# Attention row sums on one Trainium2 core: the last 64 keys added by GpSimd instead of multiplied by TensorE

## Chip, core and metric

The kernel runs on one core of a Trainium2 chip. The metric is the device time of one execution in microseconds (us), here 455.82, the median of 3 runs (454.74 to 456.12). Engines are named as in the profile: PE is TensorE's matmul, PEld its weight load, ACT is ScalarE, DVE is VectorE, POOL is GpSimd, SP is SyncE.

## What is computed

```python
scores = cap * np.tanh(scale * np.matmul(q, k.transpose(0, 1, 3, 2)) / cap)   # 8 batches x 12 heads, 448 x 448, head size 64
attn = np.exp(scores - max)
attn = attn / (np.sum(attn, axis=-1, keepdims=True) + 1e-09)
x = np.matmul(attn, v)                      # then reordered to 3584 tokens x 768
idx = np.argmax(x @ w_gate, axis=1)         # 8 experts
for e in range(8):                          # the 80 tokens of expert e with the largest gate weight
    out[tok] = gate_w[tok] * (np.maximum(x[tok] @ w1[e], 0.0) @ w2[e])
```

## The kernel before

Attention is cut into 24 units of four heads: two pairs `pr` of two heads `h`. Keys lie on the partitions and queries on the free axis. Of a head's 448 keys, three chunks of 128 fill the partitions. The last 64 keys would fill only half of them, so their exps are folded (`rest_of`, L1154): the first 224 queries stand on partitions 0 to 63, the other 224 on partitions 64 to 127. All exps of a unit lie in one tile `e`: slots 0 and 1 hold the folded rests of both pairs, the next twelve the chunks.

The program is one list of steps. The 25 passes of the loop `for w in range(NU + 1)` (L1488) run the scores and exps of unit w and, interleaved with them, the values and sums of unit w-1. I call such a pass step w. Its order is written out by hand in the string `STEPS` (L1470); `FIRST` and `LAST` are the lists of the first and the last step.

- `q0` to `q6` (`scores`, L1160): `q0` multiplies the folded rests, `q1` to `q6` one chunk of one pair each. Every score pass ends with a tanh on ACT (L1180), which reads the two-bank buffer `sc`. There are two such buffers.
- `e3`, `e0`, `e1`, `e2` (`expo`, L1182): the exps of slots `RUNS`, in place, on ACT (L1184). `e3` is the rests, `e0` and `e1` hold pair 0 and the first chunk of pair 1, `e2` the last two chunks of pair 1.
- `p00`, `p01`, `p10`, `p11` (`esum`, L1186): POOL adds the three chunks of a pair into a tile `t` of 128 partitions x 2 heads x 448 queries, two chunks first (L1191), then the third (L1194), one instruction of 448 elements for each head. The pool of `t` has three buffers.
- `v0` to `v6` (`av`, L1205): passes over the previous unit. A pass works on two halves of 64 rows at once (`half`, L1196): rows 0 to 63 and rows 64 to 127 of the array each multiply 64 keys into a bank of their own, `av_0`, `av_1` or `sp`. `PASSES` (L1473) names them. In `v3` rows 0 to 63 and in `v4` rows 64 to 127 sum the tiles `t` into `sp` with matmuls against ones ("s" there, L1213); the first of them in `v3` is where PE first needs the tiles.
- `r0`, `r1`, `r2` (`rests`, L1233): the last 64 keys, with 224 queries a matmul. Rows 0 to 63 give the first half of the queries, rows 64 to 127 the second. A pass multiplies either by `v` into an `av` bank (L1246) or by ones into `sp` (L1244): `r0` is av_0 and `sp`, `r1` is `sp` and av_1, `r2` is av_1 and av_0.
- `s` (`sums`, L1249) on DVE transposes `sp` and takes reciprocals; `n0`, `n1` (`scaled`, L1262) multiply the `av` banks by them, which frees these banks for the next `v0`.
- `b` (`background`) places pieces of the routing (gates, ranks, lists of tokens) between the steps. A planner with a clock of its own decides how many; `PLACE` (L51) tells it what time the six places of a step stand for.

```python
f = ((0, None), (None, 1), (1, 0))[part][i]
if f is None:
    behind(nc.tensor.matmul(st["sp", u][...], ones[w, 0:32], e, start=(part == 0), stop=False))
else:
    behind(nc.tensor.matmul(st["av", u, f][...], last_of(u, pr, h, i)[w, 32 * f:32 * f + 32], e, ...))
```

Unit 23 (`DIRECT`) has no tiles `t`: its chunks are summed by PE (`total_of`). After attention, from about 327 us on, the experts' matmuls stream 84 loads of weights.

Of the kernel before, what the change touches and what calls it, by code (L numbers as in the profile page):

```python
# [7 lines left out]
F32 = mybir.dt.float32  # L8
# [3 lines left out]
ALU = mybir.AluOpType  # L12
# [4 lines left out]
B, H, S, D = 8, 12, 448, 64  # L17
# [3 lines left out]
CK = 128  # L21
# [26 lines left out]
WPRE = 8  # L48
WMORE = 10
DIRECT = (23,)  # L50
PLACE = (2650, 1500, 1500, 1880, 2250, 1880)  # L51
SUMS = (1500, 6200)
VALUES = (1880, 2650)
LASTPLACE = (3950, 6200, 2650, 1300, 1300, 1300)
# [11 lines left out]
HQ = S // 2  # L66
# [54 lines left out]
def attn_moe(ctx, tc, q2, k, v, cap, wg, w1, w2, capacity, ct, out):  # L121
    nc = tc.nc
# [15 lines left out]
    ones = consts.tile([128, 128], F32, name="ones")  # L138
# [951 lines left out]
    st = {"laid": set(), "banks": ["misc"], "held": {}, "take": None, "read": 0, "late": False}  # L1090
# [29 lines left out]
    with ExitStack() as a2:  # L1120
        ep = a2.enter_context(tc.tile_pool(name="ep", bufs=2, reuse_waits="tile"))
        tp = a2.enter_context(tc.tile_pool(name="tp", bufs=3, reuse_waits="tile"))
# [28 lines left out]
        def last_of(u, pr, h, i):  # L1151
            return st["v", u][:, pr, h, NK] if h == i else st["vx", u][:, pr]

        def rest_of(u, pr, h):  # L1154
            return st["e", u][:, h, HQ * pr:HQ * pr + HQ]

        def chunk_of(u, pr, c, h):
            return st["e", u][:, 2 + 2 * NK * pr + 2 * c + h]

        def scores(u, x):  # L1160

            if ("e", u) not in st:
                st["e", u] = ep.tile([CK, 2 + 4 * NK, S], F32, name=f"e{u}", tag="e")
            ps = pss.tile([CK, 2, 512], F32, name=f"sc{u}_{x}", tag="sc")
            if x == 0:
                for pr in range(2):
                    for m in range(4):
                        for h in range(2):
                            w = slice(64 * h, 64 * h + 64)
                            i, y = m // 2, NK * CK * (1 - h) + 32 * (m % 2)  # L1170
                            nc.tensor.matmul(ps[32 * m:32 * m + 32, h, HQ * pr:HQ * pr + HQ], st["k", u][w, pr, y:y + 32], st["q", u][w, pr, HQ * i:HQ * i + HQ],  # L1171
                                             start=True, stop=True)
            else:
                pr, c = divmod(x - 1, NK)
                for m in range(4):
                    for h in range(2):
                        w = slice(64 * h, 64 * h + 64)
                        y = KR * h + c * CK + 32 * m
                        nc.tensor.matmul(ps[32 * m:32 * m + 32, h, :S], st["k", u][w, pr, y:y + 32], st["q", u][w, pr], start=True, stop=True)  # L1179
            nc.scalar.activation(st["e", u][:, 2 * x:2 * x + 2], ps[:, :, :S], AF.Tanh, scale=st["regs"][0])  # L1180

        def expo(u, x0, x1):  # L1182
# [2 lines left out]

        def esum(u, pr, i):  # L1186
            e = st["e", u][:, 2 + 2 * NK * pr:2 + 2 * NK * (pr + 1)]
            if i == 0:
                t1 = st["es", u, pr] = tp.tile([CK, 2, S], F32, name=f"t1{u}_{pr}", tag="t1")
                for h in range(2):  # L1190
                    nc.gpsimd.tensor_tensor(t1[:, h], e[:, h], e[:, 2 + h], op=ALU.add)  # L1191
            else:
                for h in range(2):
                    nc.gpsimd.tensor_tensor(st["es", u, pr][:, h], st["es", u, pr][:, h], e[:, 4 + h], op=ALU.add)  # L1194

        def half(u, i, what):  # L1196

            w = slice(KR * i, KR * i + KR)
            if what == "s":
                return [(st["sp", u], ones[w, 0:32], st["es", u, g // 2][w, g % 2], False, i == 1) for g in range(4)]  # L1200
            f, c = what
            return [(st["av", u, f], st["v", u][w, g // 2, g % 2, c, 32 * f:32 * f + 32], chunk_of(u, g // 2, c, g % 2)[w],
                     c == 0 and f == i, c == NK - 1 and f != i) for g in range(4)]

        def av(u, n):  # L1205

            if n == 0:
                for f in range(2):
                    st["av", u, f] = psa.tile([128, 512], F32, name=f"av{u}_{f}", tag=f"av{f}")
            todo = [half(u, i, x) for i, x in enumerate(PASSES[n]) if x != "s" or u not in DIRECT]  # L1210
            for g in range(4):
                for ps, v_, e, first, final in [x[g] for x in todo]:
                    behind(nc.tensor.matmul(ps[32 * g:32 * g + 32, :S], v_, e, start=first, stop=final))  # L1213

        def behind(mm):

            if st.get("turned"):
                tc.add_manual_dep(mm.ins, st.pop("turned").ins.name, SYNC, reason="rows of the array change banks")
            st["mm"] = mm
# [13 lines left out]
        def rests(u, part):  # L1233

            if part == 0:
                st["sp", u] = ps1.tile([128, 512], F32, name=f"sp{u}", tag="sp")
            for g in range(4):
                pr, h = divmod(g, 2)
                for i in range(2):
                    w = slice(KR * i, KR * i + KR)  # L1240
                    f = ((0, None), (None, 1), (1, 0))[part][i]
                    e = rest_of(u, pr, h)[w]
                    if f is None:
                        behind(nc.tensor.matmul(st["sp", u][32 * g:32 * g + 32, HQ * i:HQ * i + HQ], ones[w, 0:32], e, start=(part == 0), stop=False))  # L1244
# [222 lines left out]
            nc.tensor.matmul(ready[:, 0:128], ones, ones, start=True, stop=True)  # L1467
        guards()
        setup()
        STEPS = ("q0 q1 e3 v0 r0 b q2 v1 b q3 e0 v2 x b q4 p00 r1 v3 x b q5 e1 v4 s v5 p01 l b q6 e2 r2 v6 p10 p11 n0 n1 b").split()  # L1470
        FIRST = "q1 q2 q3 e0 q4 p00 q5 e1 p01 l q6 e2 p10 p11 q0 e3".split()
        LAST = ("v0 r0 q v1 v2 b x q r1 v3 t x q s b v4 v5 r2 v6 n0 n1 b q b q b q b").split()
        PASSES = (((0, 0), (1, 0)), ((0, 1), (1, 1)), ((0, 2), (1, 2)), ("s", (0, 0)), ((1, 0), "s"), ((1, 1), (0, 1)), ((1, 2), (0, 2)))  # L1473
        TURNS = (0, 1, 2, 3, 4, 5, 6)
# [13 lines left out]
        for w in range(NU + 1):  # L1488
# [7 lines left out]
            if w == NU:  # L1496
                transfers(w)
                st["gates"] = None
            todo = FIRST if w == 0 else STEPS if w < NU else LAST
            st["late"] = w == NU  # L1500
            left = 1 + -w % NQ
            for i, x in enumerate(todo):
                k_ = x[0]
                a_ = [int(y) for y in x[1:]]
                if k_ == 'q' and w < NU:
                    scores(w, TURNS[a_[0]])
                elif k_ == 'q':
                    begin()
# [176 lines left out]
```

## Time and profile before

| what | value |
|---|---|
| median of 3 runs | 455.82 us |
| the profiled execution's own time | 456.44 us |
| its span, first to last instruction | 454.7 us |
| granted clock of TensorE, mean | 0.987 |
| busy: PE, ACT, POOL, DVE | 432.4, 331.4, 246.4, 233.8 us |
| bytes moved, mean rate | 101.22 MB, 223 GB/s |

The profile shows one execution. Its time beside the span is 456.44 - 454.7 = 1.74 us. Busy shares are taken over the whole span, and they mix attention (up to about 327 us) with the experts. What a change in a step of attention is worth has to be read from that step: which engine waits there, for whom, and which wait ends last. On PE eight matmuls run side by side (two row halves by four column groups of 32), so a matmul's own duration is longer than the time that a pass of sixteen takes; the pace of PE is read from the starts of the passes. ACT and POOL instructions of one engine overlap a little too, so their pace is also read from start to start.

### The profile page before, as it was taken

The page shows a single profiled execution, that of the slowest core. Times are in us where ns is not written, and L with a number is a line of the kernel's source. Part 1 is how long each engine was busy: PE and PEld are TensorE (multiplying, and loading weights), DVE is VectorE, ACT ScalarE, POOL GpSimd, SP SyncE. Part 2 cuts the span into 40 slices and gives each one's busy share as a digit, 9 for nine tenths or more (in the row PEclk, how much of TensorE's full clock was granted, in tenths as well). Part 3 has the DMA queues.
Part 4 walks back from the last instruction along what each step waited for, and adds up shares of the span by engine and source line. Part 5 has one row for each costly group of instructions (what it writes and reads, how often), then busy time and mean ns, then how long its engine had stood idle before and what let it go on. Part 6 is the DMA issues. An engine that isn't in the chain of part 4 may idle for free.

```text
span 454.7 us, 21513 instructions
## 1 busy us (share of the span) xinstructions
PE 432.4 (95%) x9533; PEld 230.3 (51%) x9533; DVE 233.8 (51%) x756; ACT 331.4 (73%) x386; POOL 246.4 (54%) x277
## 2 busy tenths in 40 slices
PE   7899999999999999999999999999899999989990
PEld 4344544654444444445444544544346766677680
DVE  1033345337534563776259897977855886210002
ACT  5999989989998988897889988879601154257142
POOL 1767766767765675765576766857655110331000
PEclk9899999999999999999999999999999999999996
DMA  6667695697769559863834862874839997999961
GB/s 158 176 176 203 198 268 160 180 288 211 204 179 269 155 162 276 234 187 99 229 88 133 219 176 82 245 207 147 241 107 360 409 414 275 308 368 410 411 253 38
DMA packets 70549, 101.22 MB, mean 223 GB/s; under 512 B 15264, under 2 KB 52896, under 8 KB 70448
## 3 DMA queue, kind: packets, MB, share of 16 engines
q1 hardware_dynamic: 69072, 96.31, 67.9%
q0 software_dynamic: 752, 3.26, 2.3%
q8 instruction: 77, 1.26, 1.2%
q10 hardware_dynamic: 624, 0.18, 0.2%
q14 instruction: 24, 0.20, 0.1%
HBM read 76.13 MB, written 23.90 MB: 220 GB/s over the span
## 4 chain that ended last, share of the span: by engine, by line
PE 75%; DVE 10%; DMA 7%; ACT 3%; issue 2%; POOL 1%; SPq 1%; POOLq 0%; DVEq 0%; ACTq 0%
PE av L1213 22%; PE sc L1179 22%; PE hp L865 6%; PE yp L865 5%; PE sp L1213 4%; PE av L1246 3%; PE sc L1171 3%; DMA w<-in_w_dram 2%; PE sp L1244 2%; PE lgp L1292 2%; DVE gb L515 2%; DMA xge<-xs,gi 1%; PE pd L447 1%; PE hp5a L865 1%; DMA vr<-in_v_dram 1%
## 5 line engine op out<-in xcount | busy, mean ns | idle before, releaser
L1180 ACT ACTIVATE e<-sc 128x896 f32<-128x896 f32 x168 | 150.9, 913 | 31.1 <-PE sc L1179 28.8
L1213 PE MATMUL av<-e,vr 64*32 64x448 f32 x2304 | 164.5, 538 | 2.0 <-DMA vr<-in_v_dram 1.2
L1179 PE MATMUL sc<-qt,kt 64*32 64x448 f32 x2304 | 143.6, 544 | 3.1 <-ACT e L1180 2.7
L1191 POOL TENSOR_TENSOR t<-e 128x448 f32<-128x448 f32 x92 | 104.7, 1159 | 75.1 <-ACT e L1184 75.1
L1184 ACT ACTIVATE e<-e 128x1792 f32<-128x1792 f32 (+1 forms) x96 | 144.7, 1507 | 0.8
L1194 POOL TENSOR_TENSOR t<-t,e 128x448 f32<-128x448 f32 x92 | 104.5, 1158 | 31.9 <-ACT e L1184 31.9
L1213 PEld LDWEIGHTS av<-e,vr 64*32 64x32 f32 x2304 | 54.4, 107 | 61.6 <-issue 40.6
L1179 PEld LDWEIGHTS sc<-qt,kt 64*32 64x32 f32 x2304 | 42.2, 106 | 47.3 <-issue 32.3
L1254 DVE STREAM_TRANSPOSE st<-sp 128x448 f32<-128x448 f32 x24 | 15.6, 650 | 68.4 <-PE sp L1213 65.2
L1246 PE MATMUL av<-e,vr 64*32 64x224 f32 x384 | 46.6, 349 | 0.0
L1213 PE MATMUL sp<-t,ones 64*32 64x448 f32 x368 | 45.2, 536 | 0.0
L901 POOL DMA_INDIRECT out_dram<-ysv,si x6 | 6.7, 1111 | 69.2 <-ACT ysv L900 62.6
L865 PE MATMUL hp<-w,xt 128*32 128x256 f32 x720 | 41.7, 380 | 1.1 <-DVE xt L693 1.1
L865 PE MATMUL yp<-w,thv 128*32 128x192 f32 x960 | 40.8, 326 | 1.7 <-DMA w<-in_w_dram 1.7
L1246 PE MATMUL av<-e,vx 64*32 64x224 f32 x384 | 42.1, 349 | 0.0
L900 ACT ACTIVATE ysv<-yp,gq 32x192 f32<-32x192 f32 x60 | 24.8, 413 | 16.3 <-PE yp L865 7.9
L865 PEld LDWEIGHTS yp<-w,thv 128*32 128x32 f32 x960 | 32.0, 110 | 9.1 <-issue 2.5
L1266 DVE TENSOR_TENSOR x<-av,r 128x448 f32<-128x448 f32 x48 | 27.7, 618 | 14.4 <-PE av L1213 14.4
L865 PEld LDWEIGHTS hp<-w,xt 128*32 128x32 f32 x720 | 23.5, 110 | 16.3 <-issue 2.3
L1246 PEld LDWEIGHTS av<-e,vr 64*32 64x32 f32 x384 | 22.4, 107 | 16.6 <-issue 15.7
L441 DVE TENSOR_SCALAR_CACHE_REDUCE gb<-krow,kc 112x896 bf16<-112x896 f32 (+7 forms) x36 | 29.8, 871 | 0.6 <-PE pd L447 0.6
L1244 PE MATMUL sp<-e,ones 64*32 64x224 f32 x384 | 28.4, 349 | 0.0
(254 smaller groups left out, 443.0 us busy)
## 6 DMA issues: line engine op xcount, KB each, us to landing
w<-in_w_dram SPq DMA_DIRECT2D x36, 512.0 KB, 8.5
w<-in_w_dram SPq DMA_DIRECT2D x48, 384.0 KB, 8.1
vr<-in_v_dram SPq DMA_DIRECT2D x24, 512.0 KB, 3.9
out_dram<-zero SPq DMA_DIRECT2D x14, 768.0 KB, 5.4
xs<-xb SPq DMA_DIRECT2D x32, 336.0 KB, 6.2
kt<-in_k_dram SPq DMA_DIRECT2D x46, 224.0 KB, 5.4
qt<-in_q_dram SPq DMA_DIRECT2D x46, 224.0 KB, 5.3
vx<-in_v_dram SPq DMA_DIRECT2D x48, 32.0 KB, 3.7
```

The source lines that it names most:

```text
L441: nc.vector.tensor_scalar(g, krow[:, x:y], kp, 0.0, op0=ALU.is_ge, op1=ALU.add, accum_out=a)
L865: nc.tensor.matmul(spot(ps, g, q)[32 * j:32 * j + 32], of(g), w[:, q * j:q * j + q], start=(kk == 0 and g % 2 == 0), stop=(kk == last and ...
L900: nc.scalar.activation(dst, src, AF.Copy, scale=gate(g))
L1179: nc.tensor.matmul(ps[32 * m:32 * m + 32, h, :S], st["k", u][w, pr, y:y + 32], st["q", u][w, pr], start=True, stop=True)
L1180: nc.scalar.activation(st["e", u][:, 2 * x:2 * x + 2], ps[:, :, :S], AF.Tanh, scale=st["regs"][0])
L1184: nc.scalar.activation(e, e, AF.Exp, scale=st["regs"][1])
L1191: nc.gpsimd.tensor_tensor(t1[:, h], e[:, h], e[:, 2 + h], op=ALU.add)
L1194: nc.gpsimd.tensor_tensor(st["es", u, pr][:, h], st["es", u, pr][:, h], e[:, 4 + h], op=ALU.add)
L1213: behind(nc.tensor.matmul(ps[32 * g:32 * g + 32, :S], v_, e, start=first, stop=final))
L1244: behind(nc.tensor.matmul(st["sp", u][32 * g:32 * g + 32, HQ * i:HQ * i + HQ], ones[w, 0:32], e, start=(part == 0), stop=False))
L1246: behind(nc.tensor.matmul(st["av", u, f][32 * g:32 * g + 32, HQ * i:HQ * i + HQ], last_of(u, pr, h, i)[w, 32 * f:32 * f + 32], e, start=Fa ...
L1266: nc.vector.tensor_tensor(st["x", u][:, f], st["av", u, f][:, :S], st["r", u], op=ALU.mult)
```

## The change

Units 0 to 20 (`TURNED = 21`) no longer multiply the last 64 keys' exps by ones. POOL adds them into the tiles `t`, which PE sums anyway. The rests of partitions 64 to 127 belong to queries 224 to 447. So that they meet their own queries in columns 0 to 223 of `t`, the upper 64 partitions of every chunk hold the queries' halves exchanged: `flipped` reads `q` with its halves in the order second, first for the column groups that write partitions 64 to 127, and reads `e` or `t` back in that order for rows 64 to 127.

- `r0` of these units is av_0 and av_1, `r1` is empty, `r2` is as before. `sp` is begun by the first half of "s".
- POOL's adds of both heads become one instruction of 896 elements. There are new adds `p02` and `p12` of 2 x 224 elements for the rests. Pair 1 begins with `p12`, so its `p10` becomes two adds, one for each half of the queries.
- Units 21 and 22 keep `r1` and have no rests in `t`, but their adds are of 896 elements too.
- `PLACE` gives the planner 380 ns less at its fourth place.

```diff
-PLACE = (2650, 1500, 1500, 1880, 2250, 1880)
+TURNED = 21
+PLACE = (2650, 1500, 1500, 1500, 2250, 1880)
...
+        def flipped(u, i, a):
+            return a.rearrange("p (a b) -> p a b", a=2)[:, ::-1] if i and u < TURNED else a
...
-                        nc.tensor.matmul(..., st["k", u][w, pr, y:y + 32], st["q", u][w, pr], start=True, stop=True)
+                        nc.tensor.matmul(..., st["k", u][w, pr, y:y + 32], flipped(u, m // 2, st["q", u][w, pr]), start=True, stop=True)
...
         def esum(u, pr, i):
             e = st["e", u][:, 2 + 2 * NK * pr:2 + 2 * NK * (pr + 1)]
-            if i == 0:
-                t1 = st["es", u, pr] = tp.tile([CK, 2, S], F32, name=f"t1{u}_{pr}", tag="t1")
-                for h in range(2):
-                    nc.gpsimd.tensor_tensor(t1[:, h], e[:, h], e[:, 2 + h], op=ALU.add)
+            rest = st["e", u][:, 0:2, HQ * pr:HQ * pr + HQ]
+            lo, hi = slice(0, HQ), slice(HQ, S)
+            def add(to, x, y):
+                nc.gpsimd.tensor_tensor(to, x, y, op=ALU.add)
+            if ("es", u, pr) not in st:
+                st["es", u, pr] = tp.tile([CK, 2, S], F32, name=f"t1{u}_{pr}", tag="t1")
+                first = True
             else:
-                for h in range(2):
-                    nc.gpsimd.tensor_tensor(st["es", u, pr][:, h], st["es", u, pr][:, h], e[:, 4 + h], op=ALU.add)
+                first = False
+            t = st["es", u, pr]
+            if i == 2:
+                if u < TURNED:
+                    add(t[:, :, lo], e[:, 0:2, lo] if first else t[:, :, lo], rest)
+                    st["with", u, pr] = first
+            elif i == 0 and st.get(("with", u, pr)):
+                add(t[:, :, hi], e[:, 0:2, hi], e[:, 2:4, hi])
+                add(t[:, :, lo], t[:, :, lo], e[:, 2:4, lo])
+            elif i == 0:
+                add(t, e[:, 0:2], e[:, 2:4])
+            else:
+                add(t, t, e[:, 4:6])
...
-                return [(st["sp", u], ones[w, 0:32], st["es", u, g // 2][w, g % 2], False, i == 1) for g in range(4)]
+                return [(st["sp", u], ones[w, 0:32], flipped(u, i, st["es", u, g // 2][w, g % 2]), u < TURNED and i == 0, i == 1) for g in range(4)]
...
-            return [(st["av", u, f], st["v", u][...], chunk_of(u, g // 2, c, g % 2)[w],
+            return [(st["av", u, f], st["v", u][...], flipped(u, i, chunk_of(u, g // 2, c, g % 2)[w]),
...
-                    f = ((0, None), (None, 1), (1, 0))[part][i]
+                    if u < TURNED and part == 1:
+                        continue
+                    f = ((0, None if u >= TURNED else 1), (None, 1), (1, 0))[part][i]
...
-        STEPS = ("q0 q1 e3 v0 r0 b q2 v1 b q3 e0 v2 x b q4 p00 r1 v3 x b q5 e1 v4 s v5 p01 l b q6 e2 r2 v6 p10 p11 n0 n1 b").split()
-        FIRST = "q1 q2 q3 e0 q4 p00 q5 e1 p01 l q6 e2 p10 p11 q0 e3".split()
+        STEPS = ("q0 q1 e3 v0 r0 b q2 v1 b q3 e0 v2 x b q4 p00 p02 r1 v3 x b q5 e1 v4 s v5 p01 p12 l b q6 e2 r2 v6 p10 p11 n0 n1 b").split()
+        FIRST = "q1 q2 q3 e0 q4 p00 q5 e1 p01 l q6 e2 p10 p11 q0 e3 p02 p12".split()
```

Only PE's and POOL's instructions change; the orders of ACT, DVE and SP are the same before and after. PE has 4282 matmuls before and 4114 after: 21 times the 8 of `r1`. In the names below `av_0`, `av_1`, `sp` are the banks, `sc_4` is the buffer of `q4`, `t_0` and `t_1` are the tiles of pair 0 and 1, `e` are exps, `vr` and `vx` values, and the last number is a counter. On PE, in step 2, from `q4` to the sums of `v3`, this stands before:

```order
L1179 MATMUL sc_4_601<-qt_305,kt_306 32x448 x8
L1244 MATMUL sp_554<-e_311,ones 32x224
L1246 MATMUL av_1_545<-e_311,vx_465 32x224
L1244 MATMUL sp_554<-e_311,ones 32x224
L1246 MATMUL av_1_545<-e_311,vr_464 32x224
L1244 MATMUL sp_554<-e_311,ones 32x224
L1246 MATMUL av_1_545<-e_311,vx_465 32x224
L1244 MATMUL sp_554<-e_311,ones 32x224
L1246 MATMUL av_1_545<-e_311,vr_464 32x224
L1213 MATMUL sp_554<-t_0_408,ones 32x448
L1213 MATMUL av_0_544<-e_311,vr_464 32x448
```

The same place after the change:

```order
L1184 MATMUL sc_4_590<-qt_303,kt_304 32x448 x8
L1233 MATMUL sp_543<-t_0_406,ones 32x448
L1233 MATMUL av_0_533<-e_309,vr_455 32x448
L1233 MATMUL sp_543<-t_0_406,ones 32x448
L1233 MATMUL av_0_533<-e_309,vr_455 32x448
L1233 MATMUL sp_543<-t_1_453,ones 32x448
```

The eight matmuls of `r1` are gone, and `v3`, whose fifth matmul needs `t_1`, follows right behind `q4`. On POOL one unit (unit 1) was this:

```order
L1191 TENSOR_TENSOR t_0_408<-e_311 128x448 x2
L1194 TENSOR_TENSOR t_0_408<-t_0_408,e_311 128x448 x2
L1191 TENSOR_TENSOR t_1_497<-e_311 128x448 x2
L1194 TENSOR_TENSOR t_1_497<-t_1_497,e_311 128x448 x2
```

The same unit after the change:

```order
L1197 TENSOR_TENSOR t_0_406<-e_309 128x896
L1197 TENSOR_TENSOR t_0_406<-t_0_406,e_309 128x2x224
L1197 TENSOR_TENSOR t_0_406<-t_0_406,e_309 128x896
L1197 TENSOR_TENSOR t_1_453<-e_309 128x2x224 x2
L1197 TENSOR_TENSOR t_1_453<-t_1_453,e_309 128x2x224
L1197 TENSOR_TENSOR t_1_453<-t_1_453,e_309 128x896
```

Eight adds of 448 elements became three of 896 and four of 2 x 224, and five of these seven now stand behind `e1`.

## Rows read from the trace of the kernel before

**Rows 1.** Page part 1: busy us (share of the span) x instructions of each engine.
```profile
PE 432.4 (95%) x9533; PEld 230.3 (51%) x9533; DVE 233.8 (51%) x756; ACT 331.4 (73%) x386; POOL 246.4 (54%) x277
```

**Rows 2.** Waits, whole span: engine, line, whom it waited for: us, times, longest.
```profile
POOL t L1191 <- ACT e L1184: 75.1, 46, 9.4
...
POOL t L1194 <- ACT e L1184: 31.9, 23, 1.9
ACT e L1180 <- PE sc L1179: 28.8, 47, 2.5
```

**Rows 3.** Groups by line and shape: count | busy us, mean ns | idle before.
```profile
L1191 POOL TENSOR_TENSOR t<-e 128x448 f32<-128x448 f32 x92 | 104.7, 1159 | 75.1 <-ACT e L1184 75.1
...
L757 POOL TENSOR_TENSOR rh<-oh,bo 112x288 bf16<-112x288 bf16 x1 | 0.7, 666 | 0.1
...
L762 POOL TENSOR_TENSOR rt<-tab,bo 112x48 bf16<-112x48 bf16 x1 | 0.3, 264 | 0.0
```

**Rows 4.** Timeline of PE in step 3: start us, us, instruction.
```profile
41.16 0.97 PE L1171 MATMUL sc<-qt,kt 64*32 64x224 f32 x32
41.92 0.96 PE L1179 MATMUL sc<-qt,kt 64*32 64x448 f32 x16
...
43.99 0.99 PE L1179 MATMUL sc<-qt,kt 64*32 64x448 f32 x16
...
47.77 0.35 PE L1244 MATMUL sp<-e,ones 64*32 64x224 f32 x1
...
48.15 0.54 PE L1213 MATMUL sp<-t,ones 64*32 64x448 f32 x1
...
48.90 0.96 PE L1179 MATMUL sc<-qt,kt 64*32 64x448 f32 x16
...
53.04 0.97 PE L1171 MATMUL sc<-qt,kt 64*32 64x224 f32 x32
```

**Rows 5.** Timeline of ACT, from `e1` of step 2 through step 3.
```profile
38.91 1.69 ACT L1184 ACTIVATE e<-e 128x1792 f32<-128x1792 f32 x1
...
41.44 1.70 ACT L1184 ACTIVATE e<-e 128x1792 f32<-128x1792 f32 x1
43.04 1.71 ACT L1180 ACTIVATE e<-sc 128x896 f32<-128x896 f32 x2
...
46.58 0.92 ACT L1180 ACTIVATE e<-sc 128x896 f32<-128x896 f32 x1 [0.19 <-PE sc L1179]
...
48.98 1.90 ACT L1180 ACTIVATE e<-sc 128x896 f32<-128x896 f32 x2
```

**Rows 6.** Timeline of POOL, the adds `p01` and `p11` of unit 2.
```profile
40.74 2.26 POOL L1194 TENSOR_TENSOR t<-t,e 128x448 f32<-128x448 f32 x2 [1.20 <-ACT e L1184]
...
45.42 2.25 POOL L1194 TENSOR_TENSOR t<-t,e 128x448 f32<-128x448 f32 x2
```

**Rows 7.** Timelines of ACT and PE: `e1` of step 10, then step 11.
```profile
143.62 1.69 ACT L1184 ACTIVATE e<-e 128x1792 f32<-128x1792 f32 x1
...
147.75 1.71 ACT L1180 ACTIVATE e<-sc 128x896 f32<-128x896 f32 x2
...
149.70 0.98 PE L1179 MATMUL sc<-qt,kt 64*32 64x448 f32 x16
...
153.86 0.54 PE L1213 MATMUL sp<-t,ones 64*32 64x448 f32 x1
```

**Rows 8.** Timelines of DVE and POOL around step 21.
```profile
276.38 1.02 DVE L636 TENSOR_TENSOR prlh<-r,ctt 112x384 bf16<-112x384 f32 x2
...
281.28 1.16 DVE L1266 TENSOR_TENSOR x<-av,r 128x448 f32<-128x448 f32 x2 [0.72 <-PE av L1213]
...
283.43 3.98 DVE L636 TENSOR_TENSOR prlh<-r,ctt 112x384 bf16<-112x384 f32 x3
...
296.22 1.15 DVE L1266 TENSOR_TENSOR x<-av,r 128x448 f32<-128x448 f32 x2
...
285.54 2.88 POOL L1194 TENSOR_TENSOR t<-t,e 128x448 f32<-128x448 f32 x2
```

More of the change, by code (lines that the diff above doesn't have):

```diff
@@ L1178, in scores @@
                         y = KR * h + c * CK + 32 * m
-                        nc.tensor.matmul(ps[32 * m:32 * m + 32, h, :S], st["k", u][w, pr, y:y + 32], st["q", u][w, pr], start=True, stop=True)
+                        nc.tensor.matmul(ps[32 * m:32 * m + 32, h, :S], st["k", u][w, pr, y:y + 32], flipped(u, m // 2, st["q", u][w, pr]), start=True, stop=True)
             nc.scalar.activation(st["e", u][:, 2 * x:2 * x + 2], ps[:, :, :S], AF.Tanh, scale=st["regs"][0])
@@ L1199, in half @@
             if what == "s":
-                return [(st["sp", u], ones[w, 0:32], st["es", u, g // 2][w, g % 2], False, i == 1) for g in range(4)]
+                return [(st["sp", u], ones[w, 0:32], flipped(u, i, st["es", u, g // 2][w, g % 2]), u < TURNED and i == 0, i == 1) for g in range(4)]
             f, c = what
-            return [(st["av", u, f], st["v", u][w, g // 2, g % 2, c, 32 * f:32 * f + 32], chunk_of(u, g // 2, c, g % 2)[w],
+            return [(st["av", u, f], st["v", u][w, g // 2, g % 2, c, 32 * f:32 * f + 32], flipped(u, i, chunk_of(u, g // 2, c, g % 2)[w]),
                      c == 0 and f == i, c == NK - 1 and f != i) for g in range(4)]
```

## The prediction, on record before the changed kernel ran

> **What bounds the kernel now.** I read the page's busy times first, then the waits, and then one step of attention on PE, ACT and POOL side by side.
>
> PE is busy 95% of the span [rows 1], but the waits say more. ACT waits 28.8 us for scores, in 47 places, and POOL waits 107 us for exps (75.1 + 31.9) [rows 2]. So PE leads, ACT is close behind it, and POOL has room on the whole. Whether it has room at the right place is the question.
>
> Step 3 has no routing work and shows the pattern. It lasts from 41.16 to 53.04, 11.88 us [rows 4]. A pass of sixteen 448-column matmuls takes 48.90 - 48.15 = 0.75, and `r1` takes 48.15 - 47.77 = 0.38 [rows 4]. PE never stops in it for more than 0.2. ACT has almost no gap either. After the tanh of `q3` at 46.58 it runs `e0`, the tanhs of `q4` and `q5`, `e1`, the tanh of `q6`, `e2` and the tanh of the next `q0` as one chain. Its only wait is before the tanh of `q5`: the pair at 48.98 takes 1.90, where a pair without a gap takes 1.71, so 0.19 [rows 5]. And PE waits for the end of this chain. The tanh of `q0` ends at 43.04 + 0.91 = 43.95, and `q2`, which needs its buffer, starts at 43.99 [rows 4, 5].
>
> The third chain is POOL's. `e1` of step 2 ends at 38.91 + 1.69 = 40.60 [rows 5]; `p01` starts at 40.74, `p11` ends at 45.42 + 2.25 = 47.67 [rows 6], and `v3` needs it at 48.15 [rows 4]. From the end of `e1` to `v3`, which I call the lag, are 7.55 us, and 0.48 of it is spare. In step 11, which carries routing work, the lag is 153.86 - (143.62 + 1.69) = 8.55 [rows 7]. I read the two ends of the lag in the same way in the other steps. It is 7.56 in steps 2, 3 and 21; 8.02, 8.05 and 8.41 in steps 6, 18 and 19; 8.56 in 5, 8, 11 and 14; 8.87 in 9 and 12; and 9.2 to 10.5 in step 1 and the eight others.
>
> **Removed from PE.** `r1` goes in steps 1 to 21: 21 x 0.38 = 7.9 us [rows 4]. That is a ceiling. `r0` keeps its sixteen matmuls, only the bank changes, so I cost it at nothing. Per step the gain is the smaller of 0.38 and what ACT's chain allows, which is the gap before the tanh of `q5` plus the time by which the next `q2` starts after the end of its `q0` tanh. In steps 1, 2 and 20 only the gap of about 0.18 is there, as in rows 5. In step 5 it is 0.32. In the 16 others the next `q2` is held by PE and the routing (in step 11 it starts 149.70 - (147.75 + 0.91) = 1.04 after that tanh [rows 7]) or the gap itself is longer, and the whole 0.38 counts. Sum: 3 x 0.18 + 0.32 + 16 x 0.38 = 6.9 us for steps 1 to 20.
>
> **Reversed reading on PE.** The trace has no matmul that reads its queries in two stretches. The nearest row: 32 matmuls of 224 columns take 41.92 - 41.16 = 0.76, sixteen of 448 take 0.75 [rows 4]. So even a new instruction in the middle costs nothing that counts; a new stretch inside one should not cost more, and no reason makes it a gain. I take zero.
>
> **Added to POOL.** Two 448-element adds in a row take 2.25 [rows 6], one takes 1.16 [rows 3]. An add of 896 is not in the trace. It is at most the 2.25 of the pair, and at least that less one fixed cost, which is no more than the 0.26 of the 48-element add [rows 3]: 1.99 to 2.25, and I take the middle, 2.12. An add of 2 x 224 has the elements of the 448 one: from 1.10, its pace, to 1.16 + 0.26 = 1.42 if the second row began anew. I take 1.11, since the 288-element add, whose operands are read in short stretches, is not dearer per element (666/288 = 2.3 ns against 1159/448 = 2.6) [rows 3]. In all POOL gets 42 rest adds, 47 us, and saves some 8 by the merging. Its 107 us of idle time [rows 2] would cover that.
>
> But the place decides. Behind `e1` now stand `p01`, `p12`, both halves of `p10` and `p11`: 0.14 (the start after `e1`) + 2.12 + 3 x 1.11 + 0.10 (the last add needs the one before it; an estimate from the 0.07 by which two adds of 1.16 overlap in 2.25) + 2.12 + 0.06 to reach PE = 7.87 us, between 7.5 and 9.0 by the bounds. Before it was about 7.1. Without `r1` the lag that PE offers falls by 0.38, and by up to 0.2 more where ACT gains less than PE.
>
> So in steps 2 and 3 `v3` no longer waits for PE's own order but for `t_1`. It starts 7.87 - 7.56 = 0.31 later than before instead of earlier, which makes each of these steps 0.31 longer: -0.62 in place of +0.56. This is where the saved time becomes a new wait. Step 6 offers about 7.5 and loses 0.37, step 18 offers 7.67 and loses 0.20, step 19 0.04. Steps 5, 8, 11 and 14 offer 8.18, enough by 0.3. Left of the 6.9 are 6.9 - 1.18 - 0.37 - 0.24 = 5.1 us. `p00` and `p02` need 3.3 us between the ends of `e0` and `e1`, which lie at least 3.4 apart (a tanh pair of 1.71 and an `e1` of 1.69 [rows 5]), so they delay nothing.
>
> **Step 21.** Here DVE sets the time: it is busy without a gap from `x` at 281.28 to the next `x` at 296.22 [rows 8]. And DVE and POOL hold each other up. Three adds `prlh` take 3.98 beside POOL's adds, two take 1.02 while POOL rests, and POOL's own pair takes 2.88 where it takes 2.25 elsewhere [rows 6, 8]. The Trainium skill, SBUF — State Buffer, section "SBUF: two separate sides", says that GpSimd and a VectorE instruction with two SBUF inputs exclude each other for a whole instruction; by that rule a merged add would shut DVE out for twice as long at a time. The trace agrees that they do: at 0.51 an add, `prlh` alone waits 3.98 - 1.53 = 2.45 us in these rows. Unit 20 now has 1.1 x 2 more POOL work just there, and `t_1` comes about 8.9 after `e1` (7.87 and 1.0 of mutual delay), 1.3 after the old `v3`. I take 1.5 us longer for this step, from 0.3 (the PE delay is hidden by DVE) to 3.5 (three more waits of about 1.1). For the merged adds of units 21 and 22 I add 0.2.
>
> **Sum.** 5.1 - 1.5 - 0.2 = 3.4 us less. The experts' part moves with the end of attention and keeps its length: its loads wait for the buffers that attention frees. The profiled execution took 456.44, 0.62 over the median of 455.82. From 456.44 - 3.4 = 453.0, taking off the 0.62, I forecast a median of **452.4 us**; on its own this case reaches from 449 to 455.
>
> **The rivals.**
> - *PE is the bound everywhere.* If POOL's adds are quick (its chain 7.5) and ACT's gaps add up, nearly all of 7.9 us shows: 455.8 - 7.9 = 447.9. For it speaks PE's 95% [rows 1], against it the gapless ACT chain of rows 5. Chance 0.13.
> - *DVE is shut out.* The merged adds stretch the routing in steps 17 to 22, where DVE is busiest, by 3.5 in step 21 and 1 us elsewhere: 5.1 - 4.5 = 0.6 gained, 455.2. For it speaks rows 8; against it that POOL's total time, which limits such waiting, grows by about a quarter in unit 20 and not at all after it. Chance 0.15.
> - *Slower: `t_1` comes late in most steps.* It takes only dearer adds: at a POOL chain of 8.7 us (2.25 for 896 elements and 1.30 for 2 x 224) steps 2, 3, 6, 18 and 19 lose 0.83 more each, 5, 8, 11 and 14 lose 0.5, 9 and 12 lose 0.4, and step 21 0.8: 4.2 + 2.0 + 0.8 + 0.8 = 7.8, so 456.44 + 4.4 = 460.8, or 460.2 as a median. It decides from about 8.3 us on. For it speaks that the spare time was 0.48 [rows 4, 6], against it the price per element in rows 3. Chance 0.12.
> - *The reversed reading costs.* At 0.03 us a pass, some 13 passes a step, 21 steps: 8 us slower, 464. Nothing in rows 4 points to it. Chance 0.03.
>
> **How the numbers follow.** The forecast has 0.57. A measurement of this kernel can tell about 0.3%, 1.4 us. Faster by more than that: the forecast and the PE rival, 0.70. Within it: the DVE rival, 0.15. Slower: the other two, 0.15. The range takes in the PE rival below and the DVE rival above, and ends where the slower rival begins to decide: 447.8 to 457.0.
>
> **What would show it.** Right: step 3 is longer than 11.88 (about 12.2) with a wait of `v3`'s weight loads for POOL, while step 11 shrinks from 12.88 to about 12.5; POOL's busy time is about 285; an add of 896 takes about 2.1. Wrong: if step 3 shrinks to 11.5 or 11.7, my POOL chain is too long; if PE's pass is over 0.76, the reading costs; if the steps after 17 grow, it is DVE.

## The result, and the profile after the change

| | before | after |
|---|---|---|
| median (6 runs each, same chip) | 456.04 us (454.74 to 457.77) | 451.64 us (451.26 to 452.27) |
| ratio | | 0.9891, 95% interval 0.9866 to 0.9916 |
| the profiled execution's own time, its span | 456.44, 454.7 us | 451.26, 449.4 us |

The forecast was 452.4, and faster. Timed twice more on other chips, each time beside the kernel before, the same kernel gave 453.74 against 456.10 (ratio 0.9946, 0.9922 to 0.997) and 453.26 against 456.56 (0.9933, 0.9907 to 0.996). The three gains are 4.4, 2.4 and 3.3 us, so the first timing was a favourable one. Their mean, about 3.4 us, is the better figure, and it is the gain that was forecast (455.82 - 452.4).

The busy times of the page, which answer to [rows 1]:

```profile
PE 426.8 (95%) x9197; PEld 228.0 (51%) x9197; DVE 238.4 (53%) x756; ACT 329.8 (73%) x386; POOL 283.2 (63%) x247
```

PE lost 5.6 us of work, POOL gained 36.8 (283 where 285 was forecast). From the waits, over the whole span, the lines that answer to [rows 2] (engine, line, whom it waited for: us, times, longest):

```profile
POOL t L1197 <- ACT e L1189: 61.3, 39, 9.4
...
ACT e L1185 <- PE sc L1184: 27.0, 47, 2.4
...
PEld av L1233 <- DVE x L1288: 15.1, 30, 1.9
...
PEld sp L1233 <- POOL t L1197: 4.5, 9, 1.3
```

POOL's wait for exps fell from 107 to 61 us. The last line is new but for one wait of 0.4 in step 21 before: nine times the weight load of the sums waits for a tile `t`, in steps 2, 3, 5, 6, 8, 11, 14, 19 and 21. The four waits in steps 5, 8, 11 and 14, of 0.27 each, cost nothing: these steps are as long as with PE's part alone (below), where POOL adds no rests (12.93, and 12.63 three times). The groups of POOL's adds, which answer to [rows 3]; the adds of 2 x 224 are shown with their 448 elements:

```profile
L1197 POOL TENSOR_TENSOR t<-t,e 128x896 f32<-128x896 f32 x46 | 97.5, 2120 | 10.9 <-ACT e L1189 8.4
L1197 POOL TENSOR_TENSOR t<-e 128x896 f32<-128x896 f32 x26 | 55.3, 2128 | 52.5 <-ACT e L1189 52.5
L1197 POOL TENSOR_TENSOR t<-t,e 128x448 f32<-128x448 f32 x42 | 48.8, 1162 | 1.6
L1197 POOL TENSOR_TENSOR t<-e 128x448 f32<-128x448 f32 x40 | 45.4, 1157 | 0.4 <-ACT e L1189 0.4
```

An add of 896 takes 2.12, as forecast; one of 2 x 224 takes 1.16, where 1.11 was taken and 1.42 was the bound.

**Step 3**, the pattern of [rows 4 to 6]. On ACT, `e1` of step 2 ends at 38.08 + 1.69 = 39.77. Timelines of ACT, POOL, the weight loads and PE of the changed kernel, one after the other:

```profile
38.08 1.69 ACT L1189 ACTIVATE e<-e 128x1792 f32<-128x1792 f32 x1
```

```profile
39.91 2.11 POOL L1197 TENSOR_TENSOR t<-t,e 128x896 f32<-128x896 f32 x1 [0.46 <-ACT e L1189]
41.97 2.26 POOL L1197 TENSOR_TENSOR t<-e 128x448 f32<-128x448 f32 x2
44.17 3.34 POOL L1197 TENSOR_TENSOR t<-t,e 128x448 f32<-128x448 f32 x2
```

```profile
47.56 0.10 PEld L1233 LDWEIGHTS sp<-t,ones 64*32 64x32 f32 x1 [0.49 <-POOL t L1197]
```

```profile
46.19 0.96 PE L1184 MATMUL sc<-qt,kt 64*32 64x448 f32 x16
46.94 0.54 PE L1233 MATMUL sp<-t,ones 64*32 64x448 f32 x1
...
47.57 0.56 PE L1233 MATMUL sp<-t,ones 64*32 64x448 f32 x1
...
52.05 0.37 PE L1176 MATMUL sc<-qt,kt 64*32 64x224 f32 x4
52.10 0.56 PE L1233 MATMUL av<-e,vr 64*32 64x448 f32 x4
```

The third POOL line holds the second half of `p10` (448) and `p11` (896), as one group. `t_1` is complete at 44.17 + 3.34 = 47.51, and PE uses it at 47.57, 7.80 after the end of `e1`. The chain that was added up to 7.87 took 7.80. `v3` itself begins in time, at 46.94, with pair 0; only the column groups of pair 1 wait. The step is 12.08 long, 0.20 more than before; 0.31 was forecast.

How long the other steps are was read in the same way, from the start of one `q0` to the next, in every profile. The first two columns after the steps are the kernel before, in two executions; the two columns of single parts belong to experiments below.

| steps | before, twice | PE's part alone | POOL's part alone | the change, three times | forecast for the change |
|---|---|---|---|---|---|
| 2 to 4 | 37.41, 37.41 | -0.75 | +0.68 | +0.36, +0.36, +0.37 | +0.24 |
| 5 to 20 | 214.26, 214.25 | -6.58 | -0.09 | -4.76, -4.77, -4.82 | -5.16 |
| 21 | 13.56, 13.55 | +0.24 | +1.83 | +1.50, +1.45, +1.39 | +1.5 |
| 22 | 16.26, 16.26 | +0.11 | -0.10 | -0.12, -0.13, -0.14 | +0.2 with 21 |
| 2 to 22 | 281.50, 281.47 | -7.00 | +2.31 | -3.02, -3.10, -3.20 | -3.2 |
| from step 23 to the end | 143.89, 144.17 | 146.06 | 144.74 | 143.00, 144.59, 145.22 | as before |

Steps 2 to 22 repeat within 0.1 us. The part from step 23 on, which is mostly the experts, varies by 2 us between executions of one and the same kernel. That is the likely reason why the three timings differ; with one profile of each timing it is not shown.

### The profile page after: what moved, and what is told of

The parts are those of the page before. It is cut to its first block, busy times and chain, and to the rows that moved or that the text cites. A ratio compares the mean times of both kernels' runs of the same rounds, so it can differ in the third digit from the quotient of the medians.

```text
span 449.4 us, 20812 instructions
## 1 busy us (share of the span) xinstructions
PE 426.8 (95%) x9197; PEld 228.0 (51%) x9197; DVE 238.4 (53%) x756; ACT 329.8 (73%) x386; POOL 283.2 (63%) x247
## 4 chain that ended last, share of the span: by engine, by line
PE 76%; DVE 13%; ACT 4%; POOL 2%; issue 2%; DMA 2%; SPq 0%; POOLq 0%; DVEq 0%; ACTq 0%
PE av L1233 20%; PE sc L1184 19%; PE hp L866 9%; PE yp L866 9%; PE sp L1233 3%; PE av L1268 3%; PE sc L1176 2%; PE lgp L1314 2%; ACT e L1185 2%; ACT e L1189 1%; DVE prlh L637 1%; DVE x L1288 1%; DMA xge<-xs,gi 1%; DVE gb L442 1%; POOL t L1197 1%
## 5 line engine op out<-in xcount | busy, mean ns | idle before, releaser
L1233 PE MATMUL av<-e,vr 64*32 64x448 f32 x2304 | 172.2, 538 | 2.3 <-DVE x L1288 1.2
L1197 POOL TENSOR_TENSOR t<-t,e 128x448 f32<-128x448 f32 (+1 forms) x88 | 146.3, 1663 | 12.5 <-ACT e L1189 8.4
L1184 PE MATMUL sc<-qt,kt 64*32 64x448 f32 x2304 | 148.9, 540 | 3.7 <-ACT e L1185 3.0
L1197 POOL TENSOR_TENSOR t<-e 128x448 f32<-128x448 f32 (+1 forms) x66 | 100.8, 1540 | 52.9 <-ACT e L1189 52.9
L1233 PEld LDWEIGHTS av<-e,vr 64*32 64x32 f32 x2304 | 55.7, 106 | 60.1 <-issue 36.2
L1233 PE MATMUL sp<-t,ones 64*32 64x448 f32 x368 | 49.1, 538 | 0.5 <-POOL t L1197 0.5
L1268 PE MATMUL av<-e,vr 64*32 64x224 f32 x384 | 38.1, 349 | 0.0
L1268 PE MATMUL av<-e,vx 64*32 64x224 f32 x384 | 31.4, 349 | 0.0
L1297 DVE STREAM_TRANSPOSE xb<-x 128x448 f32<-128x448 f32 x48 | 27.9, 618 | 0.0
L1176 PE MATMUL sc<-qt,kt 64*32 64x224 f32 x768 | 25.1, 350 | 2.0 <-ACT e L1185 1.7
```

The lines of the kernel that those rows point to most:

```text
L1197: nc.gpsimd.tensor_tensor(to, x, y, op=ALU.add)
L1297: nc.vector.transpose(st["xt", b][:, :, j, :], st["x", u][:, f].rearrange("p (a b) -> p a b", b=32))
```

## The experiments

Eleven runs were made, on three chips, each beside the kernel before. Theory A is the prediction's: PE gives 0.38 a step as far as ACT lets it, and POOL's longer chain behind `e1` takes some of it back in steps 2, 3 and 21.

**The kernel before, once more** (no edit), for the steps' own spread.

> The kernel before, unchanged, to see step 1 a second time. In the profile of before, step 1 lasted 14.31 us and the granted clock was 0.5 in it from 15.9 to 19.3 us; in the changed kernel it lasted 12.76 at full clock. Theory A (the change shortened step 1): step 1 is again about 14.3. Theory B (chance of the clock, nothing to do with the change): with full clock there, step 1 of the kernel before is about 12.9 to 13.0, and the 1.55 us found in step 1 are no effect of the change but for some 0.2.

Measured: 455.51 us in its one execution. All steps from 2 on agree with the first profile within 0.1 us, but for 7, 9, 10 and 12, steps with routing work, which differ by 0.1 to 0.3; the sum of all is the same. Step 1 does not: 13.40 against 14.31. The last section says why.

**PE's part alone.** The adds of the rests are left out, so that POOL has no more to do than before; its other adds stay merged.

```diff
-                if u < TURNED:
+                if False:
```

> The changed kernel without the GpSimd adds of the last 64 keys (the sums of units 0 to 20 leave these keys out), all else as changed: what TensorE alone saves. Theory A (TensorE's saving is bounded by ScalarE's chain, and GpSimd's late tile costs steps 2, 3 and 21): about 7 us less than before, 449; steps 2 and 3 at 11.7 and 11.5, step 21 at about 13.5. Rival, TensorE is the bound everywhere: steps 2 and 3 both at 11.5, 8 us less. Rival, the merged adds shut VectorE out: step 21 still about 15, 5.5 us less.

Measured: 450.25 us, ratio 0.9872 (0.9839 to 0.9904). Steps 2 to 22 lose 7.0 us. Steps 2 and 3 lose 0.19 each, steps 8, 11 and 14 lose 0.25, and steps 13 and 15 to 17 lose 0.38. In steps 2 and 3, which have no routing work, ACT's chain allows half of what PE gives up, as the gap of [rows 5] said; for step 3 the whole 0.38 was expected. In steps 8, 11 and 14 what is missing is DVE's: in step 11 `v0` waits for `x`, which starts 0.95 after the step's start instead of 0.82. Step 21 is 0.24 longer, where no change was expected: its `x` starts 1.62 after the step's start instead of 0.31, which the experiments on step 21 below explain. The rival "PE is the bound everywhere" is out even for PE's part alone.

**POOL's part alone.** PE does what it did before (the queries are not exchanged either), and POOL adds zeros in the place of the rests.

```diff
...
-            rest = st["e", u][:, 0:2, HQ * pr:HQ * pr + HQ]
+            rest = zero[:, 0:HQ].rearrange("p (a b) -> p a b", a=1).broadcast_to([CK, 2, HQ])
...
-                    if u < TURNED and part == 1:
-                        continue
-                    f = ((0, None if u >= TURNED else 1), (None, 1), (1, 0))[part][i]
+                    f = ((0, None), (None, 1), (1, 0))[part][i]
```

> GpSimd's part alone: its adds as in the changed kernel, in number, shape and order, but with zeros in place of the last 64 keys, and TensorE's work as before (r0 and r1 with ones, queries not exchanged). Theory A: the lag of 7.56 that steps 2, 3 and 21 offer is too short for a chain of about 7.9, so steps 2 and 3 grow by 0.3 to 0.6 each and step 21 by 1.5, the rest stays: about 2.3 us more than before. Rival, GpSimd has room: no change. Rival, VectorE is shut out by the merged adds: steps 17 to 22 grow by 3 or more, steps 2 and 3 do not.

Measured: 459.31 us, ratio 1.0063 (1.0038 to 1.0087). It costs 2.3 us in steps 2 to 22, all of it in three places: step 3 is 0.21 longer, step 4 0.47, step 21 1.83. Elsewhere the 42 adds of rests, 42 x 1.16 = 49 us in all, cost nothing: POOL's wait for ACT covers them. Step 2 did not grow, though 0.3 to 0.6 was expected, and yet its wait is there: the sums of pair 1 begin 0.25 after those of pair 0 (39.05 and 38.80 us), and the next step still begins on time. Step 3 pays for it: its `x` starts 0.52 after the step's start, where before it is 0.31 [rows 4]; step 4 pays for step 3 in the same way, with 0.51.

This kernel also has the change's `PLACE`. Its steps 5 to 20 are as long as before, within 0.1 in all, so `PLACE` by itself gives nothing. The two parts together would give -4.7; the change gives -3.1. Of the 1.6 between them, 0.4 lies in steps 2 to 4 and 0.8 in steps 6, 7 and 18 to 20. That fits the forecast's reckoning: without `r1` PE is ready for `t_1` earlier, and the same chain on POOL costs more. Another 1.1 lies in steps 9 and 12, to which the reckoning does not apply, and step 21 gives 0.6 back. In step 9 of the change PE stands in the middle of a score pass, for nothing that the profile shows:

```profile
122.27 0.15 PEld L1184 LDWEIGHTS sc<-qt,kt 64*32 64x32 f32 x9 [0.82 <-issue]
```

Its three profiles have this stop, with 0.82, 0.74 and 0.71 us; the kernel before has one of 0.59 in its second profile; PE's part alone and the versions below that add head by head have none. Its cause stays open.

**Unit 20 not turned.**

```diff
-TURNED = 21
+TURNED = 20
```

> The changed kernel with TURNED = 20, so unit 20 is summed as before and only its adds stay merged. Theory A (step 21 grew by 1.5 because the tile of unit 20 came late): step 21 back to about 13.6, 1.4 us less than the changed kernel, ratio to before about 0.986. Rival, the merged adds shut VectorE out in step 21: it stays near 15, ratio 0.989.

Measured: 452.62 us, ratio 0.992 (0.9894 to 0.9946), against 456.05 for the kernel before on this chip. Step 21 is 14.16 instead of 15.0, and not the 13.6 that was expected; step 20 is 11.99. The sum of the two is 26.15, where the change has 27.2 and the kernel before 25.77. So one microsecond of step 21's cost is the work for unit 20, and some 0.4 is not.

**The changed kernel again, and its merging alone.** The second puts the kernel before's two adds for two heads into one, in both places, and changes nothing else.

```diff
-                for h in range(2):
-                    nc.gpsimd.tensor_tensor(t1[:, h], e[:, h], e[:, 2 + h], op=ALU.add)
+                nc.gpsimd.tensor_tensor(t1, e[:, 0:2], e[:, 2:4], op=ALU.add)
...
```

> The changed kernel once more, on the same chip as the next three. Theory A says that the change is worth what steps 2 to 22 lose in the traces, 281.5 - 278.5 = 3.0 us, and some 0.5 in step 1: a median 3 to 4 us under before on a second chip, ratio 0.992, with steps 2, 3 and 21 again at about 12.05, 12.08 and 15.06 and the experts' part anywhere between 143 and 146. Rival: the 4.4 us of the first timing are all due to the change, because the experts' part became 0.9 shorter; then it is again at 143.0 and the ratio 0.989.

> The kernel before with merged adds alone: one GpSimd add of 896 elements for each pair of 448, nothing else. Theory C (the merging alone makes VectorE late): steps 2 to 18 as before, step 21 at about 14.1 instead of 13.56. Rival, the merging is free: all steps as before; steps 2 and 3 are 11.88 in both.

Measured: 453.74 us for the changed kernel (ratio 0.9946, where 0.992 was expected), with the steps of its first profile but another length of the experts' part. So the rival that the first 4.4 us were all the change's is out. Merging alone gave 457.34 in its one execution; steps 2 to 20 are 0.2 shorter than before, and step 21 is 14.75, 1.19 longer. There `v0` waits, in the timeline of the weight loads of the merged kernel:

```profile
281.98 0.13 PEld L1211 LDWEIGHTS av<-e,vr 64*32 64x32 f32 x2 [1.01 <-DVE x L1264]
```

DVE's `x` comes 1.24 after the step's start instead of 0.31, since DVE had to wait for longer adds. From this I formed a rival: step 21 is slow because of the merging, and not because of the late `t_1`.

**Three units left out.** Units 1, 2 and 20 are not turned (every `u < TURNED` becomes `u in TURNED`); the second version also adds head by head from unit 18 on.

```diff
-TURNED = 21
+TURNED = frozenset(range(21)) - {1, 2, 20}
...
```

> The changed kernel without units 1, 2 and 20, which are summed as before but with merged adds. Theory A (late tiles cost in steps 2, 3 and 21): steps 2 and 3 at 11.88 each, 0.37 less together than the changed kernel, step 21 at 14.2 as with TURNED = 20. In all some 1.3 us under the changed kernel. Rival, the exchange itself or something else than the wait costs in steps 2 and 3: they stay at 12.05.

> As the kernel without units 1, 2 and 20, and from unit 18 on the adds of 896 elements are again two of 448, one for each head. Theory C (with TURNED = 20 step 21 still took 14.16 and not 13.56, because in steps 19 and 20 VectorE waits 2.0 us for one add of 896 where it waited 1.1 for one of 448): step 21 back to 13.5 to 13.6, so 0.6 less than without this edit. Rival, the rest adds of units 18 and 19 are what makes VectorE late: step 21 stays near 14.2. Steps 19 and 20 may grow by 0.1 to 0.2.

Measured: 452.29 us (ratio 0.9911, 0.9882 to 0.9941) and 452.51 (0.9919, 0.989 to 0.9948), on the chip where the changed kernel gave 453.74. Their steps 2 to 22 take 276.20 and 276.07, 2.3 us less than the changed kernel's 278.40. Of that, 0.55 is steps 2 to 4 (37.22 instead of 37.77), and 1.0 and 1.6 are steps 20 and 21. Step 9 gives 0.5 and 0.8, mostly because the stop described above is missing; in the second version step 19 takes 0.5 back. Step 2 stayed at 12.07 where 11.88 was expected, and step 3 fell to 11.87. It is not the rival's exchange, for neither unit that step 2 works on is turned here. After the gain of step 1, which unit 0 gives, step 2 begins 0.38 after the end of `e1` and not 0.57 as before; that this makes it longer is likely, not shown. Step 4 got back its 0.38 (13.28 against 13.64).

**Late `t_1` or merging, in step 21.** All 21 units turned, head by head from unit 18 on.

```diff
-                nc.gpsimd.tensor_tensor(to, x, y, op=ALU.add)
+                if u >= 18:
+                    for h in range(2):
+                        nc.gpsimd.tensor_tensor(to[:, h], x[:, h], y[:, h], op=ALU.add)
+                else:
+                    nc.gpsimd.tensor_tensor(to, x, y, op=ALU.add)
```

> The changed kernel with one edit: from unit 18 on POOL's adds are issued one head at a time again (448 or 224 elements), with all 21 units still turned. It asks what makes step 21 1.5 us longer. If it is the merged instructions of 896 elements, which hold up DVE for their whole length, step 21 falls from 15.0 to about 13.9 and steps 19 and 20 stay within 0.3, so some 1 us less than the changed kernel, about 452.7 on its chip of the run before. If it is the late tile t_1 of unit 20 (the prediction's mechanism), step 21 stays at about 15, since by head the same work stands behind e1, and the time is that of the changed kernel.

Measured: 453.9 us, ratio 0.9945 (0.9925 to 0.9964). Step 21 grew to 15.95, where the late tile was to leave it at about 15 and the rival at 13.9. Both missed. Steps 20 and 21 together, from the profiles:

| | merged adds | head by head |
|---|---|---|
| unit 20 turned | 27.19 | 27.78 |
| unit 20 not turned | 26.16 (three units left out) | 25.56 |

Turning unit 20 costs 1.0 with merged adds and 2.2 without. (With step 19 added, the two fields of the second row are equal, 40.1: there merging costs nothing.) In step 21 of the changed kernel the weight loads of the sums wait for the tile, and so they do, longer, where the adds go head by head (second fence):

```profile
284.21 0.10 PEld L1233 LDWEIGHTS sp<-t,ones 64*32 64x32 f32 x1 [1.29 <-POOL t L1197]
```

```profile
283.70 0.10 PEld L1237 LDWEIGHTS sp<-t,ones 64*32 64x32 f32 x1 [1.89 <-POOL t L1199]
284.79 0.10 PEld L1237 LDWEIGHTS sp<-t,ones 64*32 64x32 f32 x1 [0.95 <-POOL t L1199]
```

But DVE sets the time of this step, and whether it waits for these sums is read from `st`, its first instruction on them. DVE's timeline, of the changed kernel and then of the head-by-head kernel:

```profile
276.68 1.16 DVE L1288 TENSOR_TENSOR x<-av,r 128x448 f32<-128x448 f32 x2
...
287.91 0.17 DVE L618 COPY offo<-offp 112x8 f32<-112x8 f32 x1
287.99 0.64 DVE L1276 STREAM_TRANSPOSE st<-sp 128x448 f32<-128x448 f32 x1
...
291.84 1.15 DVE L1288 TENSOR_TENSOR x<-av,r 128x448 f32<-128x448 f32 x2
```

```profile
285.11 0.75 DVE L618 COPY offo<-offp 112x8 f32<-112x8 f32 x1
287.29 0.65 DVE L1280 STREAM_TRANSPOSE st<-sp 128x448 f32<-128x448 f32 x1 [1.42 <-PE sp L1237]
...
289.28 1.10 DVE L305 TENSOR_TENSOR d<-mx,lg 112x32 f32<-112x32 f32 x1
290.41 1.08 DVE L308 SCALAR_TENSOR_TENSOR cand<-d,ctt 112x32 f32<-112x32 f32 x1
```

In the changed kernel `st` stands right behind `offo`, and DVE has no gap from one `x` to the next. So PE's wait for `t_1` lies in the shadow of DVE and costs nothing here. Head by head, `st` waits 1.42 for the sums, and `d` and `cand` meet two adds (they take 0.84 and 0.19 in the changed kernel). Read from the timelines in this way (us):

| kernel | `x` starts after step 21's start | from this `x` to the next | DVE's gap before `st` (none: under 0.1) |
|---|---|---|---|
| before | 0.31 | 14.94 | none |
| merging alone | 1.24 | 15.09 | none |
| the change | 1.48 | 15.16 | none |
| unit 20 not turned, merged adds | 1.61 | 14.16 | none |
| the change, head by head from unit 18 on | 0.31 | 17.10 | 1.42 |
| three units left out, head by head | 0.31 | 15.11 | none |

So the 1.5 us of step 21 in the change are 1.17 by which `x` is late when the step begins, 0.22 from `x` to `x`, and 0.13 by which the next `x` stands earlier in step 22. The late `x` comes with the merged adds: every version that has them around unit 19 shows it, with `t_1` of unit 20 late or not, and no version with adds head by head does. The microsecond that turning unit 20 costs with merged adds (15.16 against 14.16) is in DVE's own instructions, since DVE has no gap in either kernel. Only head by head does a late `t_1` set the time.

**Half of two units.** Units 1 and 2 turned for pair 0 alone, whose rests POOL adds between `e0` and `e1`; unit 20 not at all; head by head from unit 18 on. The changed kernel ran beside it.

```diff
-TURNED = 21
+TURNED = frozenset((u, pr) for u in range(20) for pr in range(2)) - {(1, 1), (2, 1)}
...
-                    if u < TURNED and part == 1:
+                    if (u, pr) in TURNED and part == 1:
...
```

> Units 0 and 3 to 19 turned as in the change, units 1 and 2 for pair 0 alone (their r1 keeps the four matmuls of pair 1), unit 20 not at all, adds by head from unit 18 on. Pair 0's rests are added between e0 and e1, so nothing new stands behind e1 in steps 2 and 3. If the POOL chain behind e1 is what made these steps longer, they are 11.69 to 11.88 each here (before 11.88, changed 12.05 and 12.08), and the whole is as good as the version with three units left out, or up to 0.4 us better: about 452.1 to 452.5, some 1.4 us below the changed kernel. If adding anything to POOL in these units costs, step 3 is over 12 again. Rival on the half pass: if the four matmuls of the half r1 take as long as the eight, steps 2 and 3 are 11.88.

> The changed kernel once more beside the other two, since two chips gave it 0.989 and 0.995 of before. By the step lengths attention is 3.0 us shorter each time, and what differs is the experts' part (143.0 against 144.6). If that is chance from one execution to the next, this gives a ratio between the two, about 0.992 (452.5), with steps 2 to 22 at 278.4 again. If the first run's 4.4 us were the true gain, it gives 451.6.

Measured: 452.2 us (ratio 0.9903, 0.987 to 0.9937) against 453.26 for the changed kernel. Steps 2 and 3 are 11.69 and 11.84, with nothing waiting for POOL, so the chain behind `e1` is what made them 12.05 and 12.08. But step 4 is 13.62 again, and steps 2 to 4 take 37.16, only 0.06 less than with units 1 and 2 left out. Its `x` starts 0.66 after the step's start, instead of 0.31. PE's timeline of step 3 shows where that comes from:

```profile
46.86 0.54 PE L1237 MATMUL sp<-t,ones 64*32 64x448 f32 x1
...
46.90 0.35 PE L1270 MATMUL sp<-e,ones 64*32 64x224 f32 x1
...
47.08 0.35 PE L1270 MATMUL sp<-e,ones 64*32 64x224 f32 x1
...
47.27 0.54 PE L1237 MATMUL sp<-t,ones 64*32 64x448 f32 x1
```

Pair 0's column groups begin the sums at 46.86, while pair 1's first do their half of `r1` (46.90 and 47.08) and come to the sums at 47.27, some 0.4 later, as much as the whole `r1` took [rows 4]. Half the matmuls of a pass do not halve its time, for the column groups that still have work.

The three versions without unit 20 and with less in units 1 and 2 (452.2 to 452.5) are below the changed kernel of their chip by 1.1 to 1.5 us, and below the kernel before by about 4. By medians they beat both; the intervals of their ratios overlap with the changed kernel's, but the steps, which repeat within 0.1 us, say 2.3 us of attention.

## Why the prediction was right

**PE's gain.** 6.9 us were forecast for steps 1 to 20. PE alone gave 7.3 in steps 2 to 20, which is close, but in part by luck. Step 3 gave 0.19 and steps 8, 11 and 14 gave 0.25 where the whole 0.38 was counted. Steps 7, 9, 10 and 12 gave 0.59 to 0.72 each, more than the 0.38 that was called a ceiling; they are the steps that differ between two executions of the kernel before.

**The chain on POOL.** 7.87 forecast, 7.80 measured, of durations that were forecast within 0.05. The new wait appeared where it was said, in steps 2, 3 and 21, and in six more, of which four cost nothing.

**What those waits cost.** Here two terms were mis-sized, though the sum hardly shows it. Steps 2 and 3 were to grow by 0.31 each and step 4 to gain its 0.38, +0.24 in all. They grew by 0.17 and 0.20, step 4 gained 0.02, and the sum is +0.36. The wait hits only pair 1's column groups. They stay behind to the step's end: in the timeline above, the next `q0` begins at 52.05 while the last `av` matmuls of the other groups start at 52.10. `x` needs these banks complete. DVE's rows, of the changed kernel and of the kernel before:

```profile
52.73 1.16 DVE L1288 TENSOR_TENSOR x<-av,r 128x448 f32<-128x448 f32 x2 [0.74 <-PE av L1233]
```

```profile
53.35 1.16 DVE L1266 TENSOR_TENSOR x<-av,r 128x448 f32<-128x448 f32 x2 [0.72 <-PE av L1213]
```

`x` starts 52.73 - 52.05 = 0.68 into step 4 where it started 53.35 - 53.04 = 0.31 [rows 4], and `v0` follows it. So part of the wait in one step is paid in the next, and a step's length does not show the whole price. Leaving units 1 and 2 out brought step 4 back to 13.28, which shows it, as do steps 3 and 4 of POOL's part alone.

**Steps 5 to 20** gave 4.8 of the 5.16. Steps 6 and 18 were to lose 0.37 and 0.20 to POOL. Step 18 lost 0.19. Step 6 itself lost 0.06 (0.25 gained, against 0.31 with PE's part alone), but step 7 paid for it: its `x` starts 0.67 after its start, where it is 0.31 with PE's part alone, and the step is 0.36 longer (13.64 against 13.28). The three steps at 0.25 took 0.4, step 20 kept 0.0 to 0.1 of its 0.18. Steps 7, 9, 10 and 12 gave 1.5 together, as counted, but as 0.2, -0.1, 0.7 and 0.7 (first profile): here too the sum is luck.

**Step 21** was forecast at +1.5 and measured at 1.4 to 1.5. The size is luck, for the mechanism was another in part. The wait for `t_1` is there, a little longer than forecast (the tile is used 9.4 us after the end of `e1`, where 8.9 was reckoned), but DVE covers it: from `x` to `x` the step grew by 0.22, which is the lower bound that was stated for this case (0.3, "the PE delay is hidden by DVE"). The rest is the late `x` that the merged adds bring, for which the forecast had nothing in this step. What held of the forecast is that DVE sets the time, that GpSimd's adds hold it up, and that the work for unit 20 costs: 1.0. Step 22 cost nothing, against 0.2; the last unit with merged adds, 22, is summed in step 23 and can't be told from the experts' part.

**The rest.** The experts' part kept its length on the average (144.3 against 144.0). In the five kernels that shorten attention by 4 us or more in steps 2 to 22 it was 145.5 to 146.1. Whether some of an earlier end of attention is given back there, by the stream of weights, was not tried and stays open.

Of the rivals, "DVE is shut out" had the right mechanism for most of step 21, at a price of 1.2 us in one step and not 4.5; "`t_1` late in most steps" needed a chain of 8.3, and it is 7.8; the reversed reading costs nothing, as the sixteen matmuls of `q4`, half of which read so, take 46.94 - 46.19 = 0.75 like before [rows 4].

## What to carry to other kernels

When work moves to an idle engine, add up that engine's instructions between the event that releases them and the one that needs them, and compare with the spare time step by step: 49 us of added adds took back less than 4 of the 7 us here: 1.1 in steps 2 to 4, 0.4 in 6 and 7, 0.7 in 18 to 20, 1.2 in 21, and most of the rest in step 9, for a cause that stays open. Then leave out the steps that lose most. Read the step behind a new wait too: what is late in one step can be paid in the next. And before a wait is called the cause of a longer step, look whether the engine that sets the step's time waits for what comes of it.

## What the runs showed beside that

- **GpSimd's longer adds hold VectorE longer.** In step 21, `prov` and `prrh` took this in the kernel before, and then in the changed one:

```profile
287.34 1.27 DVE L643 TENSOR_TENSOR prov<-rev,cms 112x160 bf16<-112x160 f32 x1
288.64 2.01 DVE L646 TENSOR_TENSOR prrh<-prov,prpay 112x480 bf16<-112x480 bf16 x2
```

```profile
282.13 2.21 DVE L644 TENSOR_TENSOR prov<-rev,cms 112x160 bf16<-112x160 f32 x1
284.38 2.84 DVE L647 TENSOR_TENSOR prrh<-prov,prpay 112x480 bf16<-112x480 bf16 x2
```

  `prov` alone takes 0.31 where POOL rests (merging alone, a little later in its step). Beside adds of 448 it waits about one of them, beside adds of 896 about 1.9 us. The rule of the Trainium skill that the prediction named (SBUF — State Buffer, section "SBUF: two separate sides") fits: the wait grows with the length of the add.
- **A stretch at half clock.** In the first profile of the kernel before, PE was granted 0.50, 1.2 GHz, from 15.9 to 19.3 us; in the second and in the changed kernel 1.00, 2.4 GHz. The tables by stretch, of the first profile of the kernel before and of the changed kernel (us, busy time of PE, PEld, DVE, ACT and POOL, PEclk, DMA share, GB/s):

```profile
12.00:15.00 3.00, 1.55 (x49) 0.55 (x34) 0.12 (x1) 2.97 (x4) 1.98 (x3) 1.00 0.94 241
15.90:19.30 3.40, 3.27 (x54) 1.19 (x46) 0.00 (x0) 3.27 (x4) 3.16 (x4) 0.50 0.94 244
```

```profile
12.00:15.00 3.00, 1.44 (x48) 0.50 (x32) 1.51 (x4) 2.97 (x4) 1.82 (x2) 1.00 1.01 269
15.90:19.30 3.40, 2.91 (x81) 1.40 (x89) 0.00 (x0) 3.37 (x5) 2.93 (x3) 1.00 0.95 221
```

  PE had been half idle in both just before. The stretch cost 0.9 us of step 1 (14.31 against 13.40), so the two profiles differ by that much more than the change explains; its own gain in step 1 is 0.4 to 0.65. Of the other profiles only that of POOL's part alone had such a stretch too, at 0.51 from 17.2 to 24.0, and its step 1 took 16.38.
- **An operand read in two stretches in reversed order costs TensorE nothing**: 0.75 us for sixteen matmuls of 448 columns, whether all read straight on or half of them in reversed order.
